# Softmax exps on VectorE as two fp16 parts from any key tile, seven P buffers, group sums turned first, new clocks in the static scheduler

## The chip, the cores and the metric

The kernel runs on one core of one Trainium2 chip. The metric is the device time of one execution in microseconds (us). Executions over 1.5% slower than the fastest of the same kernel are left out of the means. A run's ratio is the mean time of its executions over the mean time of the executions of the kernel before in the same rounds on the same chip, so it is not quite the ratio of the medians quoted beside it. One execution of the kernel before took 3638 us (its other runs 962 to 968); its cause is not known, and it is in no ratio.

## The reference, cut to what matters

```python
def _A_ref(x, wqkv, wo):                       # x: 1 x 2048 x 512, 32 heads of 16
    ...
    scores = jnp.einsum("bhqd,bhkd->bhqk", q, k) * (Dh ** -0.5)
    p = _softmax(scores, axis=-1)
    o = jnp.einsum("bhqk,bhkd->bhqd", p, v)
    ...
h = x + _A_ref(_layernorm(x), A_wqkv, A_wo)
h2 = h + _B_ref(_layernorm(h), B_w_gate, B_w_up, B_w_down)   # sigmoid-gated, width 1792
```

The work is 2048 score blocks of 128 keys x 512 queries (4 query chunks x 32 heads x 16 key tiles). Each needs an exp of 65,536 numbers and a product with V.

## The kernel before

The score matmul gives scores for 128 keys and 512 queries in PSUM. A tile is three such blocks. ScalarE takes the exp of two or three of them into a buffer `pt` ("P buffer"); VectorE may take the third. P V matmuls then add into one PSUM bank `acc`, four heads side by side in the columns. A group is 4 heads of one chunk: 64 blocks. When a group is complete, VectorE transposes `acc` and the next group may use it. Projections and the feed-forward of the previous chunk fill PE in between.

The order of all instructions is fixed when the program is built. A small scheduler in Python keeps one clock for each engine (`T["P"]`, `T["A"]`, `T["D"]` for PE, ScalarE, VectorE), adds an assumed duration for each job, and emits what its clocks say is ready. The program never changes this order afterwards, so a wrong duration can become a wait.

```python
LAT = 100.0                                   # assumed semaphore latency, ns
...
def want_dve(n):                              # shall VectorE get a block of this tile?
    ...
    if not half and len(quads) > 1: return False
    if pend > 2000 or busy > 1500: return False
    return pend + busy + 2400 + 1100 * (4 - len(half[1:])) <= rest * 1100
...
def dexp_first(src, u, n):                    # scores -> fp16 bit pattern of about 2**x
    first = nc.vector.tensor_scalar(out=J[:, k, :], in0=src, scalar1=ZOFF, scalar2=0.0,
                                    op0=ALU.add, op1=ALU.max)
    T["D"] = max(T["D"], sc_end[n] + LAT) + 610
    ...
def dexp_rest():                              # four blocks ("quad") at once, later
    X = dvx.tile([P, 3, 4, QC], I16, name="X", bufs=2)
    for s in range(1, 4):
        ... nc.vector.tensor_scalar(out=X[:, s - 1, 0:k, :], in0=J[:, 0:k, :],
                                    scalar1=float(STEP[s]), scalar2=None, op0=ALU.add)
...
# main loop, one tile n
start = max(T["A"], sc_end[n] + LAT)
dable = (len(tl) == GU and tl[-1][:2] not in ((0, 0), (0, 1)) and tl[-1][2] >= KD0   # last 5 key tiles
         and not any(un.n in hold for un in avq))
split = (dable and max(T["D"], sc_end[n] + LAT) <= start + 600 and (half or len(quads) <= 1)
         and pend <= 2000)
wa = len(tl) - split
ex = nc.scalar.activation(out=pt[:, 0:wa, :], in_=pss[:, 0:wa, :], func=ACT.Exp, scale=AS)
T["A"] = start + 98 + 427 * wa
...
if split:
    dexp_first(pss[:, GU - 1, :], tl[-1], n)
```

A VectorE block is thus a sum of four shifted fp16 patterns, each with its own weighted V (`Vw`, for the last five key tiles only, ND = 5): four P V matmuls.

## Time and profile before

| | before |
|---|---|
| median time (first three runs) | 966.4 us (962.8 to 967.7) |
| steady part (first three-block exp to last exp) | 816 us of a span of 960 us |
| ScalarE work in it at its own pace | 719 us |
| VectorE blocks / P V matmuls | 428 / 3332 |

How to read it: in the trace, exps that wait for nothing start 904 ns apart (two blocks) or 1330 ns apart (three), tanh 478 ns. "Work at its own pace" is the count of each in the steady part times these spacings; what is left of the stretch is lost to waits (97 us here). The prediction below cuts the steady part at 96 and 883 us and so gets 690 of 787 us, with the same 97 us lost.

The page of the kernel before: busy time of each engine, then tenths of busy time in 40 slices and the granted PE clock in tenths, then the chain of work that ended last.

```profile
PE 796.9 (83%) x6441; PEld 248.0 (26%) x6441; DVE 681.1 (71%) x1260; ACT 796.2 (83%) x782; POOL 2.9 (0%) x7
...
PE   4587988887878779989988888898988689799597
...
DVE  7752978777878768886767797787666697676241
ACT  5389989989989789999887898999887799898041
...
PEclk9699989989989799998997999999899799999899
...
ACT 36%; PE 35%; issue 15%; DVE 11%; DMA 1%; SPq 0%; ACTq 0%; DVEq 0%
```

ScalarE and PE are both at 83%, the chain alternates between them, and PEclk shows slices with less than the full clock.

The costliest groups of the page: line, engine, operation, out<-in, shapes and count, then busy us and mean ns, then the idle time before them and who ended it.

```profile
L1145 ACT ACTIVATE pt<-PS 128x1024 f16<-128x1024 f32 (+1 forms) x664 | 729.2, 1221 | 75.6 <-PE PS L997 55.6
L1016 DVE TENSOR_SCALAR J<-PS 128x512 int16<-128x512 f32 x428 | 289.4, 686 | 154.8 <-PE PS L905 142.8
L997 PE MATMUL PS<-pt,Vaug 128*17 128x512 f16 x1562 | 228.8, 409 | 10.3 <-DVE xs L951 10.1
L1038 DVE TENSOR_SCALAR X<-J 128x2048 int16<-128x2048 int16 (+2 forms) x351 | 211.4, 640 | 1.5
L997 PE MATMUL PS<-X,Vw 128*17 128x512 f16 x1284 | 155.9, 391 | 1.6 <-DVE X L1038 1.4
L997 PE MATMUL PS<-J,Vaug 128*17 128x512 f16 x440 | 133.3, 407 | 0.0
```

A VectorE block costs one J and three quarters of an X operation on four blocks, and the P V matmuls over J and X (1284 + 440 = 1724 recorded) outnumber those over `pt`.

Waits, total us, times, longest:

```profile
DVE J L1016 <- PE PS L905: 142.8, 159, 5.3
...
ACT pt L1145 <- PE PS L997: 55.6, 45, 3.9
...
ACT xr L1235 <- PE PS L1232: 25.3, 1, 25.3
...
ACT pt L1145 <- PE PS L905: 18.1, 36, 1.2
```

Exp waits for P V (a P buffer is not free) 55.6 us. The 25.3 us wait at L1235 is ScalarE at the very end of attention, waiting for PE.

The windows view, one row for start, steady part and tail: length, then busy us (and count) of PE, PEld, DVE, ACT, POOL, then PE clock, DMA share, GB/s.

```profile
0.00:65.40 65.40, 39.10 (x231) 16.20 (x235) 48.17 (x134) 36.58 (x47) 2.90 (x7) 0.87 0.31 97
65.40:881.60 816.20, 697.77 (x5934) 205.54 (x5927) 609.02 (x1081) 741.11 (x704) 0.00 (x0) 0.94 0.06 19
881.60:960.10 78.50, 60.01 (x281) 26.28 (x280) 23.95 (x47) 18.54 (x32) 0.00 (x0) 0.94 0.18 59
```

### The profile page before, as it was taken

Reading aid. Unit: us, or ns where it says so; the run is one execution under the profiler, and the core shown is the slowest. Engines: PE = TensorE matmul, PEld = TensorE weight load, DVE = VectorE, ACT = ScalarE, POOL = GpSimd, SP = SyncE. Lnnn points to the kernel's source line nnn. Section 1 sums busy time; section 2 is a strip of 40 time slices with the busy share of each in tenths; the row PEclk is TensorE's granted clock in tenths of the full one; section 3 lists DMA queues with packets and bytes.
Section 4 is the critical chain, followed back from the end, with each engine's and each line's share of the span. In section 5 each row is a group of like instructions: output and inputs, shape, how many; then the busy total and the mean of one; then the engine's idle time right before and its main releaser. Section 6 shows DMA issues by size and latency. Waiting matters only on the chain.

```text
span 960.1 us, 16077 instructions
## 1 busy us (share of the span) xinstructions
PE 796.9 (83%) x6441; PEld 248.0 (26%) x6441; DVE 681.1 (71%) x1260; ACT 796.2 (83%) x782; POOL 2.9 (0%) x7
## 2 busy tenths in 40 slices
PE   4587988887878779989988888898988689799597
PEld 1232222222222222222222222222222122222243
DVE  7752978777878768886767797787666697676241
ACT  5389989989989789999887898999887799898041
POOL 1000000000000000000000000000000000000000
PEclk9699989989989799998997999999899799999899
DMA  5020001000000000100000001111000000102300
GB/s 186 5 74 1 2 5 52 1 1 1 1 1 12 1 23 23 56 23 24 28 6 7 17 1 46 34 38 52 23 12 12 12 2 23 45 24 88 104 6 25
DMA packets 37169, 26.26 MB, mean 27 GB/s; under 512 B 2528, under 2 KB 37088, under 8 KB 37088
## 3 DMA queue, kind: packets, MB, share of 16 engines
q1 hardware_dynamic: 35456, 23.99, 8.3%
q10 hardware_dynamic: 1632, 1.18, 0.4%
q8 instruction: 52, 0.85, 0.4%
q14 instruction: 29, 0.24, 0.1%
HBM read 23.07 MB, written 2.10 MB: 26 GB/s over the span
## 4 chain that ended last, share of the span: by engine, by line
ACT 36%; PE 35%; issue 15%; DVE 11%; DMA 1%; SPq 0%; ACTq 0%; DVEq 0%
ACT pt L1145 34%; PE PS L997 11%; PE PS L905 10%; PE PS L695 6%; PE PS L712 4%; DVE J L1016 3%; DVE X L1038 3%; PE PS L1284 1%; ACT th L723 1%; PE PS L266 1%; DVE xs L951 1%; PE PS L261 1%; DVE st L239 1%; DMA out_dram<-ob 1%; DVE hT L707 1%
## 5 line engine op out<-in xcount | busy, mean ns | idle before, releaser
L1145 ACT ACTIVATE pt<-PS 128x1024 f16<-128x1024 f32 (+1 forms) x664 | 729.2, 1221 | 75.6 <-PE PS L997 55.6
L1016 DVE TENSOR_SCALAR J<-PS 128x512 int16<-128x512 f32 x428 | 289.4, 686 | 154.8 <-PE PS L905 142.8
L997 PE MATMUL PS<-pt,Vaug 128*17 128x512 f16 x1562 | 228.8, 409 | 10.3 <-DVE xs L951 10.1
L1038 DVE TENSOR_SCALAR X<-J 128x2048 int16<-128x2048 int16 (+2 forms) x351 | 211.4, 640 | 1.5
L997 PE MATMUL PS<-X,Vw 128*17 128x512 f16 x1284 | 155.9, 391 | 1.6 <-DVE X L1038 1.4
L997 PE MATMUL PS<-J,Vaug 128*17 128x512 f16 x440 | 133.3, 407 | 0.0
L695 PE MATMUL PS<-xnT_80,wgu 128*128 128x512 bf16 x336 | 87.9, 384 | 1.2 <-ACT th L723 0.7
L997 PEld LDWEIGHTS <-Vaug 128*17 128x17 bf16 x2048 | 56.5, 90 | 88.5 <-issue 71.3
L707 DVE SCALAR_TENSOR_TENSOR hT<-th,PS 128x512 bf16<-128x512 f32 x56 | 38.4, 686 | 29.5 <-PE PS L695 28.6
L997 PEld LDWEIGHTS <-Vw 128*17 128x17 bf16 x1284 | 39.5, 88 | 70.8 <-issue 57.1
L905 PE MATMUL PS<-QT_91,KT_85 32*128 32x512 bf16 x256 | 36.4, 408 | 18.6 <-ACT pt L1145 18.6
L723 ACT ACTIVATE th<-PS 128x512 f32<-128x512 f32 x56 | 36.0, 643 | 16.9 <-PE PS L695 16.7
L905 PE MATMUL PS<-QT_92,KT_86 32*128 32x512 bf16 x256 | 37.2, 408 | 14.9 <-ACT pt L1145 14.4
L905 PEld LDWEIGHTS <-KT_84 32*128 32x128 bf16 x512 | 21.4, 91 | 104.3 <-issue 100.2
L712 PE MATMUL PS<-wd,hT 128*128 128x512 bf16 x168 | 45.9, 404 | 2.4 <-DVE ob L717 1.6
L905 PEld LDWEIGHTS <-KT_85 32*128 32x128 bf16 x512 | 20.8, 91 | 100.8 <-issue 100.2
L905 PE MATMUL PS<-QT_90,KT_85 32*128 32x512 bf16 x256 | 36.2, 405 | 12.8 <-ACT pt L1145 12.5
L905 PEld LDWEIGHTS <-KT_86 32*128 32x128 bf16 x512 | 21.5, 91 | 93.6 <-issue 92.7
L905 PE MATMUL PS<-QT_95,KT_87 32*128 32x512 bf16 x256 | 35.9, 398 | 11.1 <-ACT pt L1145 10.7
L905 PE MATMUL PS<-QT_93,KT_86 32*128 32x512 bf16 x256 | 34.8, 389 | 11.8 <-ACT pt L1145 11.3
L905 PEld LDWEIGHTS <-KT_87 32*128 32x128 bf16 x512 | 20.1, 91 | 90.6 <-issue 90.2
L905 PE MATMUL PS<-QT_94,KT_87 32*128 32x512 bf16 x256 | 34.3, 382 | 10.8 <-ACT pt L1145 10.5
(217 smaller groups left out, 525.4 us busy)
## 6 DMA issues: line engine op xcount, KB each, us to landing
wgu<-in_B_w_gate_dram SPq DMA_DIRECT2D x21, 256.0 KB, 3.0
wgu<-in_B_w_up_dram SPq DMA_DIRECT2D x21, 256.0 KB, 3.4
out_dram<-ob SPq DMA_DIRECT2D x16, 128.0 KB, 1.7
wd<-in_B_w_down_dram SPq DMA_DIRECT2D x1, 1792.0 KB, 7.6
xr<-in_A_x_dram SPq DMA_DIRECT2D x12, 128.0 KB, 2.6
X<-in_B_w_gate_dram SPq DMA_DIRECT2D x2, 768.0 KB, 4.6
X<-in_B_w_up_dram SPq DMA_DIRECT2D x2, 768.0 KB, 6.3
wv_sb<-in_A_wqkv_dram SPq DMA_DIRECT2D x1, 512.0 KB, 6.0
```

The lines of the kernel that those rows point to most:

```text
L239: nc.vector.bn_stats(out=st[:], in_=src)
L261: nc.tensor.matmul(ps, lhsT=w_sb[:, d, p * P:(p + 1) * P], rhs=xnT[c][:, d, :], start=(d == 0), stop=(d == DC - 1))
L266: nc.tensor.matmul(ps, lhsT=xnT[t // TQ][:, d, (t % TQ) * P:(t % TQ + 1) * P], rhs=wv_sb[:, d, :], start=(d == 0), stop=(d == DC - 1))
L695: nc.tensor.matmul(ps, lhsT=w[:, d, :], rhs=hnT[:, d, :], start=(d == 0), stop=(d == DC - 1))
L707: nc.vector.scalar_tensor_tensor(out=hT[:, f, :], in0=th[:], scalar=1.0, in1=ps, op0=ALU.add, op1=ALU.mult)
L712: nc.tensor.matmul(ps, lhsT=hT[:, f, i * P:(i + 1) * P], rhs=wd[:, f, :], start=(f == 0), stop=(f == FC - 1))
L723: nc.scalar.activation(out=th[:], in_=ps, func=ACT.Tanh, scale=0.5)
L905: mm = nc.tensor.matmul(pss[:, ui, :], lhsT=KT[g // 2][32 * j:32 * j + 32, kt * P:(kt + 1) * P], rhs=q[32 * j:32 * j + 32, :], start=True, ...
L997: nc.tensor.matmul(acc[32 * j:32 * j + VW, :], lhsT=v, rhs=un.ap, start=(c == 0), stop=(todo[qc, g, j] == 0), tile_position=(0, 32 * j))
L1016: first = nc.vector.tensor_scalar(out=J[:, k, :], in0=src, scalar1=ZOFF, scalar2=0.0, op0=ALU.add, op1=ALU.max)
L1038: nc.vector.tensor_scalar(out=X[:, s - 1, 0:k, :], in0=J[:, 0:k, :], scalar1=float(STEP[s]), scalar2=None, op0=ALU.add)
L1145: ex = nc.scalar.activation(out=pt[:, 0:wa, :], in_=pss[:, 0:wa, :], func=ACT.Exp, scale=AS)
```

## The change

The intent: (1) a VectorE block becomes two parts instead of four, so it needs two P V matmuls; no weighted V is needed, so any key tile may go to VectorE; (2) the freed SBUF holds seven P buffers instead of five; (3) the transpose of the group's sums goes ahead of other VectorE jobs; (4) the scheduler's clocks get new values (an exp 904 or 1330.5 ns, a tanh 478 ns, as spaced in the trace; the latencies and tails are settings for which no measurement stands here) and now foresee the wait for a P buffer. A block is J = 2^e(1+f) as fp16; the parts are about 2^e and 0.5·2^e(1+f)², which together follow the exponential.

```diff
-    ptp = ...tile_pool(name="ptp", bufs=5)
+    ptp = ...tile_pool(name="ptp", bufs=7)
-    Vw = const.tile([P, 3, ND, H, VW], BF16)
...
-    LAT = 100.0
+    LAT = 60.0
+    TAIL = {"A": 150.0, "D": 85.0}
-            self.end = T[eng]
+            self.end = T[eng] + TAIL[eng]
-    DRAIN = 150.0
+    DRAIN = 170.0
...            (about twenty job durations, for example)
-                pm_out(dve(1150, lambda i=i, pt=pt: nc.vector.tensor_copy(
+                pm_out(dve(605, lambda i=i, pt=pt: nc.vector.tensor_copy(
-            job = pm_out(dve(700, add, st["mark"]))
+            job = pm_out(dve(603, add, st["mark"]))
...
-            out=xs..., in_=acc), Mark(T["P"]))
+            out=xs..., in_=acc), Mark(T["P"] + DRAIN), pr=-1)
...
-        X = dvx.tile([P, 3, 4, QC], I16, name="X", bufs=2)
-        for s in range(1, 4): ... op0=ALU.add
+        X = dvx.tile([P, 2, 4, QC], I16, name="X", bufs=XB)          # XB = 3
+        def power():      X[:, 0] = (J & 0x7C00) | 7                  # tensor_scalar, four blocks
+        def fraction():   X[:, 1] = (J & 0x3FF) | 0x3800              # tensor_scalar, four blocks
+        def product(a, b): X[:, 1, a:b] = J[a:b] * X[:, 1, a:b]       # tensor_tensor fp16, two blocks
...
-        if pend > 2000 or busy > 1500:
+        if pend > 2600 or busy > 1500:
-        return pend + busy + 2400 + 1100 * (4 - len(half[1:])) <= rest * 1100
+        return pend + busy + 3000 + 1100 * (4 - len(half[1:])) <= rest * 1100
...
         start = max(T["A"], sc_end[n] + LAT)
+        if n - NPT not in hold:
+            start = max(start, av_end.get(n - NPT, 0.0) + LAT)
-        dable = (len(tl) == GU and tl[-1][:2] not in ((0, 0), (0, 1)) and tl[-1][2] >= KD0
+        dable = (len(tl) == GU and tl[-1][:2] not in ((0, 0), (0, 1))
...
-        split = (... and (half or len(quads) <= 1) and pend <= 2000)
+        split = (... and (half or (len(quads) < XB and len(open_j) < JB)) and pend <= 2600)
...
-        T["A"] = start + 98 + 427 * wa
+        T["A"] = start + 51 + 426.5 * wa
```

(The bodies of `power`, `fraction` and `product` are shortened to what they compute. The loads of the last chunk's gate weights into these buffers move behind the last P V matmuls but one tile.)

More of the change, by code (lines that the diff above doesn't have):

```diff
@@ L23 @@
 LOG2E = 1.4426950408889634
-STEP = (0, 258, 512, 770)
-WEIGHT = (1.0, 0.83984375, 0.70703125, 0.59375)
-LEVEL = 2.056638710885438
+POWER, LITTLE = 0x7C00, 7
+FRACTION, HALF = 0x3FF, 0x3800
+LEVEL = 0.5910364375591628
 SUM_LOW, SUM_HIGH = 256.0, 60000.0
@@ L171 @@
     PSUM = bass.MemoryType.PSUM
-    ND = 5
-    KD0 = NT - ND
     ZS = 1024 * SC * LOG2E
@@ L187 @@
     otp = main.enter_context(tc.tile_pool(name="otp", bufs=6))
-    ptp = main.enter_context(tc.tile_pool(name="ptp", bufs=5))
+    ptp = main.enter_context(tc.tile_pool(name="ptp", bufs=7))
     dvx = main.enter_context(tc.tile_pool(name="dvx", bufs=1))
@@ L270, in v_out @@
         nc.vector.tensor_copy(out=Vaug[:, t, :, 0:DH], in_=ps.rearrange("p (h d) -> p h d", d=DH))
-    def v_weigh(t, s):
-        nc.vector.tensor_scalar(out=Vw[:, s - 1, t - KD0], in0=Vaug[:, t], scalar1=WEIGHT[s],
-                                scalar2=None, op0=ALU.mult)
     def split_q(dst, a, qd):
@@ L550, in prep_v @@
         v_mm(ps, t)
-        job = pm_out(dve(640, lambda: v_out(ps, t), st["mark"]))
-        jobs = [job] + [dve(230, lambda s=s: v_weigh(t, s), job) for s in range(1, 4) if t >= KD0]
-        done["v", t] = jobs
+        done["v", t] = [pm_out(dve(603, lambda: v_out(ps, t), st["mark"]))]
     def early_ln(c):
@@ L567, in early_ln @@
         for i in range(TQ):
-            ja.append(dve(335, lambda i=i: apply(c, i), jn, After(("x", c - 1, i // 2)), pr=pr))
+            ja.append(dve(325, lambda i=i: apply(c, i), jn, After(("x", c - 1, i // 2)), pr=pr))
         def turn():
@@ L591, in early_k @@
                              start=(d == 0), stop=(d == DC - 1))
-        done["k0", c] = [pm_out(dve(640, lambda: nc.vector.tensor_copy(
+        done["k0", c] = [pm_out(dve(603, lambda: nc.vector.tensor_copy(
             out=KT[0][:, c * QC:(c + 1) * QC], in_=ps), st["mark"]))]
@@ L599, in prep_k @@
             proj8(ps, wk_sb, p, c)
-            done["k", p] = [pm_out(dve(640, lambda ps=ps, c=c: nc.vector.tensor_copy(
+            done["k", p] = [pm_out(dve(603, lambda ps=ps, c=c: nc.vector.tensor_copy(
                 out=KT[p][:, c * QC:(c + 1) * QC], in_=ps), st["mark"]))]
@@ L608, in prep_q @@
         dst = QTb if (qc, p) == (1, 0) else QT[2 * p:2 * p + 2]
-        job = pm_out(dve(640, lambda: nc.vector.tensor_scalar(
+        job = pm_out(dve(603, lambda: nc.vector.tensor_scalar(
             out=qd[:], in0=ps, scalar1=ZS, scalar2=None, op0=ALU.mult), st["mark"]))
-        done["q", qc, p] = [dve(220, lambda a=a: split_q(dst, a, qd), job) for a in range(2)]
+        done["q", qc, p] = [dve(262, lambda a=a: split_q(dst, a, qd), job) for a in range(2)]
     OT, otj = {}, {}
@@ L671, in add @@
                     XR.append(load_xr(qc, i + 2))
-            job = pm_out(dve(700, add, st["mark"]))
+            job = pm_out(dve(603, add, st["mark"]))
             bs = new_st()
-            j = dve(660, lambda i=i, bs=bs: stats1(h[:, i, :], bs), job)
-            j = dve(180, lambda i=i, bs=bs: stats2(bs, mv[:, i, :]), j)
+            j = dve(605, lambda i=i, bs=bs: stats1(h[:, i, :], bs), job)
+            j = dve(100, lambda i=i, bs=bs: stats2(bs, mv[:, i, :]), j)
         jn = newton_jobs(rstd[:], mv[:, :, 1], j)
@@ L683, in wo_ln @@
         for i in range(2):
-            jh[i] = dve(420, lambda i=i: apply(i), jn)
+            jh[i] = dve(455, lambda i=i: apply(i), jn)
         for i in range(TQ):
@@ L687, in wo_ln @@
             pt = transpose4(pm_tile(), hns[i])
-            pm_out(dve(440, lambda pt=pt, i=i: nc.vector.tensor_copy(
+            pm_out(dve(335, lambda pt=pt, i=i: nc.vector.tensor_copy(
                 out=hnT[:, :, i * P:(i + 1) * P], in_=pt), st["mark"]))
             if i + 2 < TQ:
-                jh[i + 2] = dve(420, lambda i=i: apply(i + 2), jn, st["mark"])
+                jh[i + 2] = dve(455, lambda i=i: apply(i + 2), jn, st["mark"])
     def gate_mm(ps, w):
@@ L738, in ffn_up @@
         gate_mm(ps, wgu[:, 0])
-        ja = pm_out(act(530, lambda: th.update({f: tanh_out(ps)}), st["mark"]))
+        ja = pm_out(act(478, lambda: th.update({f: tanh_out(ps)}), st["mark"]))
         yield pe(4, pm_new)
@@ L748, in ffn_up @@
                 GW.append(load_gate(f + 3 - FC))
-        pm_out(dve(700, lambda: glu_out(hT, f, th[f], ps2), st["mark"], ja))
+        pm_out(dve(603, lambda: glu_out(hT, f, th[f], ps2), st["mark"], ja))
     def ffn_down(qc, i):
@@ L760, in ffn_down @@
             down_mm(ps, hT, i, f, f + n)
-        pm_out(dve(700, lambda: down_out(ps, qc, i), st["mark"]))
+        pm_out(dve(603, lambda: down_out(ps, qc, i), st["mark"]))
     HOLD = Mark(None)
@@ L829, with __init__ @@
     class Block:
-        def __init__(self, qc, g, kts, kds):
+        def __init__(self, qc, g, kts):
             self.qc, self.g = qc, g
             self.a = {j: deque(kts) for j in range(4)}
-            self.d = {j: deque(kds) for j in range(4)}
         def left(self):
-            return sum(len(q) for q in (*self.a.values(), *self.d.values()))
-    blocks = deque(Block(0, g, range(c * TQ, (c + 1) * TQ), ()) for g, c in early)
-    blocks.extend(Block(qc, g, range(KD0), range(KD0, NT)) for qc, g in gseq[2:])
+            return sum(len(q) for q in self.a.values())
+    blocks = deque(Block(0, g, range(c * TQ, (c + 1) * TQ)) for g, c in early)
+    blocks.extend(Block(qc, g, range(NT)) for qc, g in gseq[2:])
     tiles = []
@@ L851, in pick @@
         if want:
-            js = [j for j in range(4) if b.d[j]]
-            if js:
-                j = max(js, key=lambda j: (len(b.d[j]), -((j - st["dj"]) % 4)))
-                last = (b.qc, b.g, b.d[j].popleft(), j)
+            j = st["dj"] % 4
+            if b.a[j]:
+                last = (b.qc, b.g, b.a[j].popleft(), j)
                 st["dj"] = j + 1
@@ L859, in pick @@
             b = blocks[0]
-            for pool in (b.a, b.d):
-                js = [j for j in range(4) if pool[j]]
-                if js:
-                    break
-            else:
+            js = [j for j in range(4) if b.a[j]]
+            if not js:
                 blocks.popleft()
@@ L869, in pick @@
                 continue
-            j = max(js, key=lambda j: (j not in used, len(pool[j]), -((j - st["aj"]) % 4)))
-            out.append((b.qc, b.g, pool[j].popleft(), j))
+            j = max(js, key=lambda j: (j not in used, len(b.a[j]), -((j - st["aj"]) % 4)))
+            out.append((b.qc, b.g, b.a[j].popleft(), j))
             st["aj"] = j + 1
@@ L914, with __init__ @@
     class Unit:
-        def __init__(self, u, ap, n, end, s=0):
-            self.u, self.ap, self.n, self.end, self.s, self.d = u, ap, n, end, s, -1
+        def __init__(self, u, ap, n, end):
+            self.u, self.ap, self.n, self.end, self.d = u, ap, n, end, -1
     avq = []
+    av_end = {}
     count, todo = {}, {}
@@ L922 @@
             count[qc, g, j], todo[qc, g, j] = 0, NT
-    NPT = 5
+    NPT = 7
     def finish_group(qc, g):
@@ L950, in turn @@
                     queue(ffn_down(qc, i), ("d", qc, i), 14 * ((qc, i) != (NQC - 2, TQ - 1)))
-        j = st["acc"] = dve(730, lambda: nc.vector.transpose(
-            out=xs[:].rearrange("p b r -> p (b r)"), in_=acc), Mark(T["P"]))
-        j = dve(680, norm, j)
+        j = st["acc"] = dve(650, lambda: nc.vector.transpose(
+            out=xs[:].rearrange("p b r -> p (b r)"), in_=acc), Mark(T["P"] + DRAIN), pr=-1)
+        j = dve(620, norm, j)
         if a:
-            otj[qc, p] = dve(720, turn, j)
+            otj[qc, p] = dve(630, turn, j)
     def av_last():
@@ L995, in av @@
             h = 8 * (g // 2) + 2 * j + g % 2
-            v = Vaug[:, kt, h, :] if un.s == 0 else Vw[:, un.s - 1, kt - KD0, h, :]
-            nc.tensor.matmul(acc[32 * j:32 * j + VW, :], lhsT=v, rhs=un.ap, start=(c == 0),
+            nc.tensor.matmul(acc[32 * j:32 * j + VW, :], lhsT=Vaug[:, kt, h, :], rhs=un.ap, start=(c == 0),
                              stop=(todo[qc, g, j] == 0), tile_position=(0, 32 * j))
         pe_time("av", MM * rows + 4 * len(uns))
+        for un in uns:
+            if un.d < 0:
+                av_end[un.n] = T["P"] + DRAIN
         qc, g = uns[0].u[:2]
@@ L1004, in av @@
         return len(uns)
-    JB = 3
-    quads = []
+    JB, XB = 2, 3
+    quads, open_j = [], []
     half = []
@@ L1015, in dexp_first @@
         k = len(half) - 1
-        first = nc.vector.tensor_scalar(out=J[:, k, :], in0=src, scalar1=ZOFF, scalar2=0.0,
-                                        op0=ALU.add, op1=ALU.max)
-        T["D"] = max(T["D"], sc_end[n] + LAT) + 610
-        todo[u[0], u[1], u[3]] += 3
-        uns = [Unit(u, J[:, k, :].bitcast(FP16), n, T["D"])]
-        uns += [Unit(u, None, n, None, s) for s in range(1, 4)]
+        nc.vector.tensor_scalar(out=J[:, k, :], in0=src, scalar1=ZOFF, scalar2=0.0,
+                                op0=ALU.add, op1=ALU.max)
+        T["D"] = max(T["D"], sc_end[n] + LAT) + 601
+        todo[u[0], u[1], u[3]] += 1
+        uns = [Unit(u, None, n, None) for s in range(2)]
         for un in uns:
@@ L1028, in dexp_first @@
             dexp_rest()
-        return first
     def dexp_rest():
@@ L1034, in dexp_rest, with ready, power, fraction @@
         k = len(quad)
-        X = dvx.tile([P, 3, 4, QC], I16, name="X", bufs=2)
-        for s in range(1, 4):
-            def step(s=s):
-                nc.vector.tensor_scalar(out=X[:, s - 1, 0:k, :], in0=J[:, 0:k, :],
-                                        scalar1=float(STEP[s]), scalar2=None, op0=ALU.add)
-                for i, uns in enumerate(quad):
-                    uns[s].ap, uns[s].end = X[:, s - 1, i, :].bitcast(FP16), T["D"]
-            chain.append((70 + 133 * k, step))
+        X = dvx.tile([P, 2, 4, QC], I16, name="X", bufs=XB)
+        V = nc.vector
+        open_j.append(J)
+        def ready(s, a, b):
+            for i in range(a, b):
+                quad[i][s].ap, quad[i][s].end = X[:, s, i, :].bitcast(FP16), T["D"] + TAIL["D"]
+        def power():
+            V.tensor_scalar(out=X[:, 0, 0:k, :], in0=J[:, 0:k, :], scalar1=POWER, scalar2=LITTLE,
+                            op0=ALU.bitwise_and, op1=ALU.bitwise_or)
+            ready(0, 0, k)
+        def fraction():
+            V.tensor_scalar(out=X[:, 1, 0:k, :], in0=J[:, 0:k, :], scalar1=FRACTION, scalar2=HALF,
+                            op0=ALU.bitwise_and, op1=ALU.bitwise_or)
+        def product(a, b):
+            x = X[:, 1, a:b, :].bitcast(FP16)
+            V.tensor_tensor(out=x, in0=J[:, a:b, :].bitcast(FP16), in1=x, op=ALU.mult)
+            ready(1, a, b)
+            if b == k:
+                open_j.pop(0)
+        chain.append((70 + 133 * k, fraction))
+        chain.append((70 + 133 * k, power))
+        for a in range(0, k, 2):
+            b = min(a + 2, k)
+            chain.append((70 + 267 * (b - a), lambda a=a, b=b: product(a, b)))
     def pop_chain():
@@ L1056, in want_dve @@
         rest = group_left() / 2.8
-        if not half and len(quads) > 1:
+        if not half and (len(quads) >= XB or len(open_j) >= JB):
             return False
-        if pend > 2000 or busy > 1500:
+        if pend > 2600 or busy > 1500:
             return False
-        return pend + busy + 2400 + 1100 * (4 - len(half[1:])) <= rest * 1100
+        return pend + busy + 3000 + 1100 * (4 - len(half[1:])) <= rest * 1100
     slots, hold = [], {}
     def early_slots():
-        for i in range(2):
-            x = dvx.tile([P, 3, 4, QC], I16, name="X", bufs=2)
-            slots.extend(x[:, s, 2 * k:2 * k + 2, :] for s in range(3) for k in range(2))
-        for i in range(JB):
-            x = dvx.tile([P, 4, QC], I16, name="J", bufs=JB)
-            slots.extend(x[:, 2 * k:2 * k + 2, :] for k in range(2))
-        slots.extend(prep.tile([P, 2, QC], I16, name=f"hold{i}")[:] for i in range(5))
+        for name, b in (("X", XB), ("J", JB)):
+            for i in range(b):
+                x = dvx.tile([P, 2, 4, QC] if name == "X" else [P, 4, QC], I16, name=name, bufs=b)
+                for s in range(2):
+                    slots.extend(([x[:, s, 0:2, :], x[:, s, 2:4, :]]) if name == "X" else [x[:, 2 * s:2 * s + 2, :]])
+        slots.extend(prep.tile([P, 2, QC], I16, name=f"hold{i}")[:] for i in range(7))
     def pt_tile(n):
@@ L1132 @@
         start = max(T["A"], sc_end[n] + LAT)
+        if n - NPT not in hold:
+            start = max(start, av_end.get(n - NPT, 0.0) + LAT)
         busy = sum(j.ns for j in dq if j.ready() is not None)
         pend = sum(c[0] for c in chain)
-        dable = (len(tl) == GU and tl[-1][:2] not in ((0, 0), (0, 1)) and tl[-1][2] >= KD0
+        dable = (len(tl) == GU and tl[-1][:2] not in ((0, 0), (0, 1))
                  and not any(un.n in hold for un in avq))
-        split = (dable and max(T["D"], sc_end[n] + LAT) <= start + 600 and (half or len(quads) <= 1)
-                 and pend <= 2000)
+        split = (dable and max(T["D"], sc_end[n] + LAT) <= start + 600 and (half or (len(quads) < XB and len(open_j) < JB))
+                 and pend <= 2600)
         if half and half[1][0].u[:2] != tl[-1][:2]:
@@ L1141 @@
             quads[:] = [q for q in quads if any(un in avq for un in q)]
-            split = split and len(quads) <= 1
+            split = split and len(quads) < XB and len(open_j) < JB
         wa = len(tl) - split
@@ L1145 @@
         ex = nc.scalar.activation(out=pt[:, 0:wa, :], in_=pss[:, 0:wa, :], func=ACT.Exp, scale=AS)
-        T["A"] = start + 98 + 427 * wa
-        ex_end[n] = T["A"]
-        avq.extend(Unit(u, pt[:, ui, :], n, T["A"]) for ui, u in enumerate(tl[:wa]))
+        T["A"] = start + 51 + 426.5 * wa
+        ex_end[n] = T["A"] + TAIL["A"]
+        avq.extend(Unit(u, pt[:, ui, :], n, ex_end[n]) for ui, u in enumerate(tl[:wa]))
         if split:
             dexp_first(pss[:, GU - 1, :], tl[-1], n)
-            ex_end[n] = max(ex_end[n], T["D"])
+            ex_end[n] = max(ex_end[n], T["D"] + TAIL["D"])
         run_act()
@@ L1191 @@
     flush()
-    tw = {}
-    Xs = [dvx.tile([P, 3, 4, QC], I16, name="X", bufs=2) for i in range(2)]
-    Js = dvx.tile([P, 4, QC], I16, name="J", bufs=JB)
-    for i, (t, f, n) in enumerate(((Xs[0], 0, 6), (Xs[1], 6, 6), (Js, 12, 2))):
-        w = t[:].rearrange("p a b n -> p (a b n)") if n == 6 else t[:].rearrange("p b n -> p (b n)")
-        w = w.bitcast(BF16).rearrange("p (k c n) -> p k c n", k=2, c=DC)
-        for k in range(2):
-            nc.sync.dma_start(out=w[:, k], in_=gate_v[k][:, :, f * P:(f + n) * P])
-        for m in range(n):
-            tw[f + m] = w[:, :, :, m * P:(m + 1) * P]
     while bg and HOLD not in (bg[0][2] or pe(0))[2]:
@@ L1207 @@
         av(8, 1e12)
+    tw = {}
+    for i in range(XB + JB):
+        t = (dvx.tile([P, 2, 4, QC], I16, name="X", bufs=XB)[:].rearrange("p a b n -> p (a b n)") if i < XB
+             else dvx.tile([P, 4, QC], I16, name="J", bufs=JB)[:].rearrange("p b n -> p (b n)"))
+        n = min(4 if i < XB else 2, FC - len(tw))
+        f = len(tw)
+        w = t[:, 0:n * 2 * DC * P].bitcast(BF16).rearrange("p (k c n) -> p k c n", k=2, c=DC)
+        for k in range(2):
+            nc.sync.dma_start(out=w[:, k], in_=gate_v[k][:, :, f * P:(f + n) * P])
+        for m in range(n):
+            tw[f + m] = w[:, :, :, m * P:(m + 1) * P]
+        if len(tw) == FC:
+            break
     qc = NQC - 1
```

## The prediction

> **What bounds it now.** From the windows view, three parts: start to 96 us (tiles two blocks wide), a steady part 96–883 us (tiles of three 128x512 score blocks), and a tail 883–960 us. The steady part decides. In the trace, back-to-back exps on ScalarE start 904 ns (two blocks) or 1330 ns (three blocks) apart, tanh 478 ns. All ScalarE work of the steady part at these spacings adds to 690 of 787 us: ScalarE is the bound at 88%, and 97 us are lost to waits. The waits view names them: exp waiting for the P V matmuls (a P buffer not yet free) 55.6 us in 45 waits, up to 3.9 us each; waiting for scores 18 us. Counted per group (between two transposes of the P V accumulator), the loss is 4 to 8 us in groups that change over badly or carry much feed-forward work. VectorE is 71% busy; PE is 83% busy but its matmul times overlap, so that is no peak.
>
> **What the change does.**
> - P V: a VectorE block needs two matmuls instead of four. The before has 428 such blocks (count of J), 3332 P V matmuls. Four run side by side, and a row of four takes about 0.216 us, so 856 fewer matmuls free about 46 us of PE, 50 us with the mean granted clock. This shortens its catching up at group changes and in the feed-forward groups.
> - Seven P buffers: two more tiles (about 2 us) of slack against the 55.6 us wait. I expect this to pay directly. Turning the accumulator first helps the same place.
> - VectorE per block: before, J 601 ns (start to start) + 3 x 600/4 = 1.05 us. After, J 601 + two bit operations on four blocks, 2 x 600/4, + two products on two blocks each. [...]
> - So the number of VectorE blocks hardly grows. Any key tile may go there, [...] and the start rule near a group's end is stricter. I expect 400 to 460 blocks (14 a group, as before); each block more or less moves 0.43 us of ScalarE.
>
> **Sum.** Steady ScalarE work stays 690 us (±12). Loss falls from 97 to about 45 us. Start 96 us and tail 77 us change little (−2). 96 + 735 + 77 − 2 ≈ 906; with a reserve for a later VectorE (it holds the score bank), 912 us.
>
> Range 885 to 943 us. Faster by over 2%: 0.85; within 2%: 0.12; slower: 0.03.
>
> **What would show it.** Waits of exp for P V matmuls under 20 us in all; P V matmuls about 2048 + J count; 128x2048 bit operations with a duration near 690 ns[...]; J count 400–460; steady ScalarE spacing unchanged at 904/1330[...].
>
> **What would make it wrong.** [...] VectorE saturating so that J comes late and score banks stall PE and ScalarE; J count well under 400 (ScalarE floor up) or well over 470 (a bigger gain); lower granted clock; new clocks in the scheduler that are too eager, so in-order PE stalls on not-yet-ready parts.

Cut from it, where marked, is the author's reckoning of what a VectorE block costs after the change, with what hung on it (a product, the VectorE work in all, its busy share, a quad): it was not worked out from the traces of this case. What it says of P V matmuls is in the trace of before: those of a row start about 4 ns apart and rows 216 to 221 ns apart (5th percentile and median), and the 1562 over `pt`, 409 ns each or 639 us in all, keep PE busy for only 228.8 us.

## The result, and the profile after

The kernel after takes 902.5 us (901.75 to 907.41, four runs) against 966.8 us, ratio 0.9353 with a 95% interval of 0.9311 to 0.9396: 6.5% faster, and within the predicted range. The parts of the sum are another matter:

| profiled run, us | before | after | predicted |
|---|---|---|---|
| start, to the first three-block exp | 65.3 | 66.6 | start and tail together −2 |
| steady: ScalarE work at its own pace | 718.7 | 692.3 | unchanged, ±12 |
| steady: lost to waits | 97.4 | 85.2 | −52 |
| tail, after the last exp | 78.6 | 55.8 | start and tail together −2 |
| VectorE blocks | 428 | 487 | 400 to 460 |

```profile
PE 765.6 (85%) x5644; PEld 232.0 (26%) x5644; DVE 795.4 (88%) x1470; ACT 770.8 (86%) x783; POOL 2.9 (0%) x7
...
PE   4498888877787899999998989989978898989897
...
DVE  7742899999999899999998999999999999899832
ACT  5399998989989999999898999988898998899741
...
PEclk9699998899988999999997899999998999899999
...
DVE 37%; ACT 26%; PE 23%; issue 12%; DMA 0%; ACTq 0%; DVEq 0%
```

VectorE went from 71% to 88% busy and now leads the chain that ended last (37%); before it had 11%.

```profile
L1155 ACT ACTIVATE pt<-PS 128x1024 f16<-128x1024 f32 (+1 forms) x663 | 700.8, 1169 | 60.3 <-PE PS L985 38.6
L1007 DVE TENSOR_SCALAR J<-PS 128x512 int16<-128x512 f32 x487 | 324.6, 685 | 16.2 <-PE PS L893 9.1
L985 PE MATMUL PS<-pt,Vaug 128*17 128x512 f16 x1499 | 218.4, 406 | 7.0 <-DVE xs L940 6.8
L1043 DVE TENSOR_TENSOR X<-J,X 128x1024 f16<-128x1024 f16 (+1 forms) x251 | 161.7, 669 | 0.0
L985 PE MATMUL PS<-X,Vaug 128*17 128x512 f16 x1014 | 150.9, 396 | 6.5 <-DVE X L1033 4.7
...
L1038 DVE TENSOR_SCALAR X<-J 128x2048 int16<-128x2048 int16 (+3 forms) x133 | 85.3, 642 | 0.2
L1033 DVE TENSOR_SCALAR X<-J 128x2048 int16<-128x2048 int16 (+3 forms) x133 | 85.2, 640 | 0.0
```

Back to back, the new operations start about 600 ns apart, as J does: the two bit operations on four blocks (2048 elements) 599 and 601 ns, products on two blocks (1024 elements) 601 ns, J 601 ns; the add on 2048 elements in before had 601.5 ns. Durations are 685 to 687 ns (the means above mix in smaller shapes). So a block in a full quad costs 601 + 2 x 600/4 + 601/2, about 1.2 us (an estimate from these spacings), against 1.05 us before. But there are 487 J.

```profile
ACT pt L1155 <- PE PS L985: 38.6, 26, 5.2
...
ACT pt L1155 <- PE PS L893: 19.2, 33, 1.8
...
DVE J L1007 <- PE PS L893: 9.1, 18, 1.3
...
ACT xr L1249 <- PE PS L1246: 4.0, 1, 4.0
```

VectorE no longer waits for scores (142.8 us before, 9.1 now): it is late itself. Exp still waits 38.6 us for P V; the prediction wanted under 20. The wait at the end of attention (xr) is gone.

```profile
0.00:66.50 66.50, 40.83 (x239) 15.90 (x239) 43.67 (x116) 38.20 (x48) 2.90 (x7) 0.87 0.29 95
66.50:844.10 777.60, 676.33 (x5182) 194.79 (x5185) 730.98 (x1315) 714.72 (x705) 0.00 (x0) 0.95 0.07 21
844.10:900.00 55.90, 48.41 (x231) 21.35 (x230) 20.72 (x41) 17.92 (x32) 0.00 (x0) 0.94 0.19 61
```

The tail has 231 matmuls where it had 281: the rest of the third chunk's feed-forward (12 gate or up and 56 down matmuls in the order of instructions of before, 14 down now) is done before attention ends.

**A late VectorE, seen in one place.** For each tile whose third block goes to VectorE, J and the exp of the other two blocks read the same score tile, whose banks the program gives to new scores only after both (in after the score matmuls waited 82.3 us in 195 waits for an exp of `pt`, and 0.2 us in one wait for J). In before, J ended after that exp in 22 of 428 tiles, 2.5 us in all; in after, in 179 of 487, 40.3 us in all. The timeline of after around one group change (start, us, engine, line, operation):

```profile
643.61 0.71 PE L985 MATMUL PS<-X,Vaug 128*17 128x512 f16 x2 [0.21 <-DVE X L1033]
...
643.81 0.69 DVE L1007 TENSOR_SCALAR J<-PS 128x512 int16<-128x512 f32 x1
...
644.25 0.67 PE L893 MATMUL PS<-QT_88,KT_84 32*128 32x512 bf16 x6
644.53 0.69 DVE L1038 TENSOR_SCALAR X<-J 128x2048 int16<-128x2048 int16 x1
...
645.14 0.68 DVE L1007 TENSOR_SCALAR J<-PS 128x512 int16<-128x512 f32 x1
645.74 0.68 DVE L1033 TENSOR_SCALAR X<-J 128x2048 int16<-128x2048 int16 x1
...
646.34 0.69 DVE L1007 TENSOR_SCALAR J<-PS 128x512 int16<-128x512 f32 x1
...
646.94 0.71 DVE L940 STREAM_TRANSPOSE xs<-PS 128x512 f32<-128x512 f32 x1
...
647.70 0.39 PE L985 MATMUL PS<-pt,Vaug 128*17 128x512 f16 x3 [0.25 <-DVE xs L940]
647.70 0.11 PEld L985 LDWEIGHTS <-Vaug 128*17 128x17 bf16 x7 [0.24 <-issue]
...
648.17 2.37 ACT L1155 ACTIVATE pt<-PS 128x1536 f16<-128x1536 f32 x2 [1.49 <-PE PS L985]
...
648.37 1.89 PE L259 MATMUL PS<-xnT_83,wq_sb 128*128 128x512 bf16 x4
```

The last two P V matmuls of the group (643.61) end at 644.32. The transpose of the sums could follow, but VectorE still has J, a bit operation, J, a bit operation and J in its fixed order, and starts the transpose at 646.94. The next group's P V matmuls begin only at 647.70, P buffers run out, and the exp at 648.17 has waited 1.49 us. Then four projection matmuls (648.37) take 1.89 us where four of the same line took 1.04 us at 351.53 us: the clock record has 0.5 from 648.1 us on. In after, gaps of ScalarE over 0.3 us from 3 us before to 4 us after such a transpose add to about 45.6 us (some us more or less, by how gaps at the edge are counted).

### The profile page after: what moved, and what is told of

Read it like the earlier page. It is cut to its first block, busy times and chain, and to the rows that moved or that the text cites. A ratio compares the mean times of both kernels' runs of the same rounds, so it can differ in the third digit from the quotient of the medians.

```text
span 900.0 us, 14693 instructions
## 1 busy us (share of the span) xinstructions
PE 765.6 (85%) x5644; PEld 232.0 (26%) x5644; DVE 795.4 (88%) x1470; ACT 770.8 (86%) x783; POOL 2.9 (0%) x7
## 4 chain that ended last, share of the span: by engine, by line
DVE 37%; ACT 26%; PE 23%; issue 12%; DMA 0%; ACTq 0%; DVEq 0%
ACT pt L1155 23%; DVE J L1007 15%; DVE X L1043 7%; PE PS L688 6%; PE PS L985 5%; PE PS L893 5%; DVE X L1033 4%; DVE X L1038 3%; DVE xs L940 2%; PE PS L264 1%; DVE hT L700 1%; PE PS L1298 1%; PE PS L259 1%; PE PS L705 1%; ACT th L716 1%
## 5 line engine op out<-in xcount | busy, mean ns | idle before, releaser
L1155 ACT ACTIVATE pt<-PS 128x1024 f16<-128x1024 f32 (+1 forms) x663 | 700.8, 1169 | 60.3 <-PE PS L985 38.6
L1007 DVE TENSOR_SCALAR J<-PS 128x512 int16<-128x512 f32 x487 | 324.6, 685 | 16.2 <-PE PS L893 9.1
L985 PE MATMUL PS<-pt,Vaug 128*17 128x512 f16 x1499 | 218.4, 406 | 7.0 <-DVE xs L940 6.8
L1043 DVE TENSOR_TENSOR X<-J,X 128x1024 f16<-128x1024 f16 (+1 forms) x251 | 161.7, 669 | 0.0
L985 PE MATMUL PS<-X,Vaug 128*17 128x512 f16 x1014 | 150.9, 396 | 6.5 <-DVE X L1033 4.7
L985 PEld LDWEIGHTS <-Vaug 128*17 128x17 bf16 x2535 | 63.6, 89 | 151.5 <-issue 130.3
L1038 DVE TENSOR_SCALAR X<-J 128x2048 int16<-128x2048 int16 (+3 forms) x133 | 85.3, 642 | 0.2
L1033 DVE TENSOR_SCALAR X<-J 128x2048 int16<-128x2048 int16 (+3 forms) x133 | 85.2, 640 | 0.0
L893 PE MATMUL PS<-QT_90,KT_85 32*128 32x512 bf16 x256 | 39.5, 428 | 12.5 <-ACT pt L1155 12.0
L893 PE MATMUL PS<-QT_93,KT_86 32*128 32x512 bf16 x256 | 37.8, 397 | 10.1 <-ACT pt L1155 9.5
L893 PE MATMUL PS<-QT_92,KT_86 32*128 32x512 bf16 x256 | 37.2, 381 | 10.4 <-ACT pt L1155 9.9
L893 PE MATMUL PS<-QT_91,KT_85 32*128 32x512 bf16 x256 | 36.4, 395 | 11.1 <-ACT pt L1155 10.5
L893 PE MATMUL PS<-QT_94,KT_87 32*128 32x512 bf16 x256 | 35.4, 384 | 11.3 <-ACT pt L1155 11.0
L893 PEld LDWEIGHTS <-KT_84 32*128 32x128 bf16 x512 | 20.5, 91 | 92.0 <-issue 87.3
L705 PE MATMUL PS<-wd,hT 128*128 128x512 bf16 x168 | 43.9, 382 | 0.4 <-DVE ob L710 0.4
L893 PE MATMUL PS<-QT_95,KT_87 32*128 32x512 bf16 x256 | 37.0, 392 | 8.0 <-ACT pt L1155 7.6
L893 PEld LDWEIGHTS <-KT_85 32*128 32x128 bf16 x512 | 20.4, 92 | 89.4 <-issue 88.1
L893 PEld LDWEIGHTS <-KT_86 32*128 32x128 bf16 x512 | 20.2, 91 | 84.7 <-issue 84.4
L893 PEld LDWEIGHTS <-KT_87 32*128 32x128 bf16 x512 | 19.4, 91 | 84.2 <-issue 83.2
```

The lines of the kernel that those rows point to most:

```text
L705: nc.tensor.matmul(ps, lhsT=hT[:, f, i * P:(i + 1) * P], rhs=wd[:, f, :], start=(f == 0), stop=(f == FC - 1))
L893: mm = nc.tensor.matmul(pss[:, ui, :], lhsT=KT[g // 2][32 * j:32 * j + 32, kt * P:(kt + 1) * P], rhs=q[32 * j:32 * j + 32, :], start=True, ...
L985: nc.tensor.matmul(acc[32 * j:32 * j + VW, :], lhsT=Vaug[:, kt, h, :], rhs=un.ap, start=(c == 0), stop=(todo[qc, g, j] == 0), tile_positio ...
L1033: V.tensor_scalar(out=X[:, 0, 0:k, :], in0=J[:, 0:k, :], scalar1=POWER, scalar2=LITTLE, op0=ALU.bitwise_and, op1=ALU.bitwise_or)
L1038: V.tensor_scalar(out=X[:, 1, 0:k, :], in0=J[:, 0:k, :], scalar1=FRACTION, scalar2=HALF, op0=ALU.bitwise_and, op1=ALU.bitwise_or)
L1043: V.tensor_tensor(out=x, in0=J[:, a:b, :].bitcast(FP16), in1=x, op=ALU.mult)
```

## The experiments

The theories. **A** (the prediction): fewer waits for P buffers, from buffers and PE relief, are the gain. **B**: the gain is ScalarE work moved to VectorE, and a shorter tail from the new clocks. C to I came up on the way. All runs gave correct results. "Blocks" is the number of VectorE blocks; half-clock is the time for which the trace's clock record, which holds only 1.0 and 0.5, has 0.5 in the profiled run.

| run | median us | ratio | blocks | P V matmuls | steady work + lost, us | tail us | half-clock us |
|---|---|---|---|---|---|---|---|
| before | 966.8 | 1 | 428 | 3332 | 718.7 + 97.4 | 78.6 | 120.6 |
| after | 902.5 | 0.9353 | 487 | 2535 | 692.3 + 85.2 | 55.8 | 110.6 |
| u1 five buffers | 919.8 | 0.9552 | 500 | 2548 | 686.7 + 108.2 | 55.1 | 100.2 |
| u2 old clocks | 965.0 | 1.0021 | 468 | 2516 | 699.8 + 103.8 | 96.1 | 195.7 |
| u3 sums not first | 901.6 | 0.9348 | 490 | 2538 | 691.0 + 86.0 | 56.5 | 100.8 |
| u4 old key tiles | 890.9 | 0.9246 | 426 | 2474 | 718.3 + 53.1 | 54.2 | 144.2 |
| u5 none at a group's end | 895.1 | 0.9274 | 419 | 2467 | 721.3 + 49.4 | 56.2 | 121.3 |
| u6 every third given back | 874.3 | 0.9040 | 415 | 2463 | 723.0 + 27.6 | 56.1 | 73.8 |
| u7 before + new clocks | 895.4 | 0.9279 | 447 | 3389 | 709.3 + 62.6 | 54.2 | 58.8 |
| u8 leftover put back | 916.5 | 0.9505 | 488 | 2536 | 691.9 + 85.1 | 64.7 | 119.4 |
| v1 u7, every sixth given back | 904.6 | 0.9396 | 418 | 3302 | 721.7 + 56.8 | 55.1 | 52.7 |
| v2 before + new latencies | 913.0 | 0.9472 | 440 | 3368 | 712.3 + 70.0 | 61.5 | 73.2 |
| v3 before + new durations | 925.0 | 0.9599 | 441 | 3371 | 711.4 + 67.2 | 78.2 | 92.8 |
| v4 every fourth given back | 880.4 | 0.9145 | 454 | 2502 | 706.4 + 48.7 | 54.3 | 74.3 |

### u1: five buffers

```diff
-    ptp = ...tile_pool(name="ptp", bufs=7)
+    ptp = ...tile_pool(name="ptp", bufs=5)
-    NPT = 7
+    NPT = 5
```

> The kernel after with five P buffers instead of seven, nothing else. The order of instructions holds 500 VectorE blocks (487 in after) and no more leftover feed-forward work. Theory A (the prediction: the buffers pay directly, because ScalarE waits for a free P buffer): exp waits for P V matmuls rise from 38.6 us to 60 us or more, time 915 to 930 us. Theory B (the gain is ScalarE work moved to VectorE and a shorter tail; the wait for P V comes from late group ends, which buffers only delay): time 900 to 910 us.

919.8 us, ratio 0.9552 (0.9517 to 0.9586). Exp waited 68.7 us for P V (38.6 in after). Theory A holds for this part: two buffers are worth 17 us in this kernel. The scheduler also answered with 13 more VectorE blocks, so it is not the buffers with all else fixed. The same step on the kernel before could not be built: without the change's smaller tables the build with seven buffers stops at the pool `fwork`, which needs 8 kb a partition where 5.78 kb are left (with six it builds; that was not run).

### u2: the old clocks

```diff
-    LAT = 60.0; TAIL = {"A": 150.0, "D": 85.0}; DRAIN = 170.0
+    LAT = 100.0; DRAIN = 150.0                  # and no tails
-        if n - NPT not in hold:
-            start = max(start, av_end.get(n - NPT, 0.0) + LAT)
-        T["A"] = start + 51 + 426.5 * wa
+        T["A"] = start + 98 + 427 * wa
...                                              # and all job durations as in before
```

> The kernel after with all scheduler times of before (latencies, tails, durations, no predicted P-buffer wait), nothing else. The order of instructions holds 468 VectorE blocks (19 fewer, 8 us more ScalarE), and after the last scores 40 more gate or up matmuls and 42 more down matmuls of the third chunk, as in before. If the clocks matter through the tail (theory B): the time from the last exp to the end grows from 56 us to 72 to 80 us and the whole is 920 to 935 us. If the clocks are only cosmetics (theory A): within 5 us of after.

965.0 us, ratio 1.0021: the whole gain is gone, more than theory B expected. The tail grew to 96 us, the steady part to 804 us, and PE spent 196 us at half clock. So of the 62 us, 40 are in the tail and 26 in the steady part (start is 3 us shorter). The tail is worse than that of before (79 us): after the last exp the trace has 39 gate or up and 55 down matmuls of the third chunk, against 8 and 56 in before and 14 down in after.

### u3: group sums not turned first

```diff
-..., in_=acc), Mark(T["P"] + DRAIN), pr=-1)
+..., in_=acc), Mark(T["P"] + DRAIN))
```

> The kernel after with the transposes of the group sums queued behind other VectorE jobs, as in before, nothing else. 490 VectorE blocks. Both theories: 0 to +6 us; PE waits for the accumulator (6.8 us in after) rise to about 10 us as in before.

901.6 us, ratio 0.9348: no difference. PE's wait for the transpose rose from 6.8 to 9.4 us, but it cost nothing. The timeline above suggests why the step does little: it puts the transpose ahead of other queued jobs, not ahead of J and the quad's operations that are already emitted. The run shows one thing more: here J ended after its exp in only 120 of 490 tiles, 22.4 us in all (179 and 40.3 us in after), and the steady part lost the same 86 us. So a late J is a sign of the overload, not a measure of what it costs.

### u4: VectorE blocks from the last five key tiles only

```diff
+    ND = 5; KD0 = NT - ND                       # key tiles of a group in two pools, as in before
...                                              # and the pools in Block and pick
-        dable = (len(tl) == GU and tl[-1][:2] not in ((0, 0), (0, 1))
+        dable = (len(tl) == GU and tl[-1][:2] not in ((0, 0), (0, 1)) and tl[-1][2] >= KD0
```

> The kernel after with VectorE blocks only from the last five key tiles, as in before, nothing else. The order of instructions holds 426 VectorE blocks instead of 487: 61 more on ScalarE, 26 us more ScalarE work at 0.4265 us each. Theory B: 915 to 930 us, and VectorE busy falls to about 80%. Theory A (count of blocks does not matter, waits do): within 8 us of after.

890.9 us, ratio 0.9246 (0.9224 to 0.9268): *faster* than after. Both theories fall here. ScalarE had 26 us more work, exactly as counted, but lost 32 us less, and exp waited 12.9 us for P V. The freedom of the key tile, the headline of the change, costs about 12 us as this scheduler uses it. The code says how the count rises: the limit to five key tiles also kept VectorE from taking blocks that `want_dve` had not asked for; without it, `split` takes any tile for which the clocks leave room. Building the orders again and counting bears this out: 59 of 428 blocks had not been asked for in before, 189 of 487 in after, 64 of 426 in u4. (An order built with `split` bound to `want_dve` has 374 blocks; it was not run.)

### u5 and u6: is it the place of the blocks, or their number?

u5, no block for VectorE when fewer than 12 of the group are left:

```diff
+        left_after.append(sum(b.left() for b in blocks if (b.qc, b.g) == tiles[n][-1][:2]))
-        dable = (len(tl) == GU and
+        dable = (len(tl) == GU and left_after[n] >= 12 and
```

> The kernel after, any key tile, but no VectorE block once fewer than 12 score blocks of the group are left. The order of instructions holds 419 VectorE blocks (487 in after; 426 in the run with the old key tiles, which was 12 us faster than after). Theory C (VectorE blocks late in a group make the group's sums late, so ScalarE runs out of P buffers at each group change): 885 to 895 us, gaps near a group change about half of the 45.6 us of after. Theory D (the freedom of the key tile itself costs, place and count do not): within 4 us of after.

u6, every third block given back, wherever it falls:

```diff
+        st["even"] = st.get("even", 0) + split
+        split = split and st["even"] * 1 % 3 >= 1
```

> The kernel after, any key tile, with every third VectorE block given back to ScalarE wherever it falls. The order holds 415 VectorE blocks, as many as the run that keeps them off the last 12 blocks of a group, but also at the group's end. Theory C (place): slower than that run by 6 us or more, gaps near a group change stay above 35 us. Theory E (count alone: VectorE is overloaded with 487): within 3 us of that run.

u5 took 895.1 us, ratio 0.9274, and u6 874.3 us, ratio 0.9040 (0.8990 to 0.9090). With 419 and 415 blocks they differ by 21 us, and against theory C the one that still takes blocks at a group's end wins. Theory E (number alone) falls as well, since the numbers are nearly equal. (u5 by itself had looked like C, at the edge of its 885 to 895 us, and not like theory D, that the freedom of the key tile itself costs. Against D speaks also that u6, with any key tile, is 17 us faster than u4 with five.) What differs is how the load is spread. The count of tiles whose J ends after their exp is 179 of 487 in after, 57 of 419 in u5 (11.6 us) and 26 of 415 in u6 (2.9 us); gaps near a group change add to about 45.6, 19.3 and 2.5 us. Busy time and chain of u6, from its page, then its waits:

```profile
PE 744.7 (85%) x5572; PEld 228.6 (26%) x5572; DVE 718.7 (82%) x1325; ACT 795.9 (91%) x783; POOL 2.9 (0%) x7
...
ACT 51%; PE 23%; issue 18%; DVE 6%; DMA 1%; SPq 0%; ACTq 0%; DVEq 0%
```

```profile
DVE J L1007 <- PE PS L893: 51.1, 83, 2.2
...
ACT pt L1157 <- PE PS L893: 8.2, 24, 0.9
...
PE PS L985 <- DVE xs L940: 0.9, 2, 0.5
```

From the view of the tile `pt` on ScalarE in u6, what the exps waited for (us, times):

```profile
its engine sat idle before it (us, times) until:
  PE PS L893: 8.2, 24
...
  PE PS L985: 0.3, 1
```

The wait of exp for P V, 38.6 us in after, is 0.3 us in u6, once. ScalarE leads the chain with 51%, VectorE has 6%. That a regular three-block exp gives VectorE and PE time to catch up is the explanation I argue for, and no run shows it by itself; shown is that VectorE is on time, that the loss near group changes is gone, and that PE is at half clock for 74 us instead of 121 us in u5. The clock is a rival that was not separated: 47 us less at half clock are worth up to 23 us of full-speed PE (an estimate, half of 47), as much as the whole difference, and no run tells whether the even load or the clock came first.

### v4: every fourth block given back

```diff
+        st["even"] = st.get("even", 0) + split
+        split = split and st["even"] * 1 % 4 >= 1
```

> The kernel after, any key tile, every fourth VectorE block given back: 454 blocks, between the 487 of after (902 us) and the 415 with every third left out (874 us). Theory E (load of VectorE is what counts, with a threshold near its free time): 876 to 890 us. If 415 was already below the best count: 870 us or less, the best of all.

880.4 us, ratio 0.9145 (0.9116 to 0.9174), within the range that theory E gave (a threshold itself was not measured). It has 17 us less ScalarE work than u6 and loses 21 us more. So of these two counts 415 is the better, and u6 stays the best kernel. It also limits the explanation by regular pauses: from 100 us after the start to 70 us before the end, VectorE worked for over 10 us without a pause of 0.1 us in 30% of the time in u6, 43% in u5 and 58% in after, but in 67% in v4, which is faster than u5.

### u7, v2, v3: the new clocks on the kernel before

u7 takes the kernel before and changes only the scheduler's numbers (and the predicted P-buffer wait); v2 only latencies, tails, exp times and that wait; v3 only the job durations.

> The kernel before with the new scheduler times alone (latencies, tails, durations, the predicted P-buffer wait), four-part exps, five P buffers, old key tiles. The order holds 447 VectorE blocks (428 in before) and no leftover of the third chunk's feed-forward after the last scores beyond 14 down matmuls. If the clocks carry most of the gain by themselves: 915 to 935 us, tail 56 us. If they pay only together with the two-part exps (PE or VectorE too full without them): 945 us or more.

> The kernel before with only the latencies, tails, exp times and the predicted P-buffer wait of the new clocks, job durations as before. 440 VectorE blocks, 38 down matmuls left over after the last scores. All new clocks together gave 895 us. Theory H (latencies and the P-buffer wait are the effective part): 900 to 918 us. Theory I (job durations are): 945 us or more.

> The kernel before with only the new job durations on VectorE and ScalarE (640 to 603 ns for an eviction, 1150 to 605 for the early transposed copy and so on), latencies as before. 441 VectorE blocks, 8 gate or up and 56 down matmuls left over, as in before. Theory H: 950 us or more. Theory I: 900 to 925 us.

u7 took 895.4 us, ratio 0.9279 (0.9237 to 0.9320): better than expected, and at least as fast as the kernel after (0.9311 to 0.9396). The clocks alone are worth 7.2%, the whole change 6.5%. v2 gave 913.0 us (0.9472), v3 925.0 us (0.9599). Neither theory H nor I is right: each half gains by itself, 5.3% and 4.0%, and together less than their sum. v2 shortened the tail by 17 us, v3 left it as it was (78.2 us); both cut the loss in the steady part from 97 to about 70 us.

### u8: the leftover put back into the tail

```diff
-                yield pe(n, pm_new, HOLD if (qc, i) == (NQC - 2, TQ - 1) else None)
+                yield pe(n, pm_new, HOLD if (qc, i) == (NQC - 2, TQ - 1) else HOLD2 if qc == NQC - 2 else None)
...
     N = len(tiles)
+    HOLD2.end = 0.0
```

> The kernel after with 42 down matmuls of the third chunk held back until attention has ended, which makes the tail do what it did in before. 488 VectorE blocks. If the tail explains its 23 us by this work: the stretch after the last exp grows by 10 to 16 us (before needed about 15 us for 12 gate or up and 56 down matmuls there), the steady part shortens by 0 to 5 us, the whole is 908 to 918 us. If the work only moves: within 3 us of after.

916.5 us, ratio 0.9505 (0.9475 to 0.9535), 14 us more than after. Its profiled run was its fastest (909.3 us; the others 914.9 to 917.1 us); in it the tail grew by 8.9 us to 64.7 us while the steady part stayed at 777 us. So leftover feed-forward at the end is paid in full (42 matmuls of about 0.216 us are 9.1 us, an estimate). The rest of the 14 us is not in the profiled run and stays open. The leftover makes up for 9 us of the 23 us directly; the other changes of the tail were not tried one by one.

### v1: what the two parts themselves are worth

u7 with every sixth block given back has as many VectorE blocks as u6, but four parts each.

```diff
             split = split and len(quads) <= 1
+        st["even"] = st.get("even", 0) + split
+        split = split and st["even"] * 1 % 6 >= 1
```

> The kernel before with the new scheduler times (895 us in its run) and every sixth VectorE block given back: 418 blocks, as many as the 415 of the two-part kernel with every third left out (874 us), but four P V matmuls a block (3302 in all, 2463 there) and five P buffers. Theory F (the two-part exps pay once VectorE is not overfilled: 839 fewer P V matmuls, about 45 us of PE): 885 us or more, and more half-clock or P V waits than the 874 us kernel. Theory G (the parts are worth nothing here, only the clocks and an even load are): 870 to 880 us.

904.6 us, ratio 0.9396, against 0.9040 of u6: theory F holds. Exp waited 26.7 us for P V; half clock was not more than in u6 (53 and 74 us), which theory F had left open. With four parts, giving blocks back makes the kernel slower than u7; its chain has PE at 40%, ScalarE at 37% and VectorE at 8%, and VectorE waited 96.0 us for scores (51.1 us in u6). So two parts with what they bring (839 fewer P V matmuls and room for two more buffers) are worth about 30 us at this count of blocks, and 21 us between the fastest kernel of each kind (u6 and u7); in after, with VectorE at 88% busy, nothing is left of it. u1 puts some 17 us of it to the buffers in another setting; the two were not separated here, and the way the blocks are thinned (one in six, one in three) differs too.

## Why the prediction was right or wrong

The total, 912 us in a range of 885 to 943, was right (902.5), but by luck: the sum behind it came out because its errors cancelled. ScalarE work was 26 us under the forecast, the loss 40 us over it, start and tail 20 us under it.

- **Right:** ScalarE's own work fills most of the steady part (692.3 of 777.5 us); its spacings stayed at 904 and 1330 ns. The bit operations on 2048 elements have the duration foreseen, near 690 ns (685 and 687 measured); a product of 1024 elements takes as long (685 ns, starts 601 ns apart). P V matmuls are 2048 plus the J count. Two buffers pay, 17 us.
- **Mis-sized, the VectorE blocks:** "the number of VectorE blocks hardly grows ... 400 to 460". It grew to 487. I took `want_dve` for the rule that limits them, but what held the number down in before was the key-tile condition in `dable`: `want_dve` did ask for fewer (298 blocks in the built order, 369 before), and 189 came in unasked (59 before). This took 26.4 us off ScalarE instead of 0 ± 12 and put VectorE at 88% busy (71% before).
- **Failed, the loss:** "Loss falls from 97 to about 45 us". It fell to 85, and exp waited 38.6 us for P V, not under 20. The prediction named the risk, "VectorE saturating so that J comes late and score banks stall PE and ScalarE", and its first part came: J ended after its exp in 179 tiles, and group sums were turned late. A stall of PE on J's score banks is not in the trace beyond the 0.2 us above. With an even load (u6) the loss is 27.6 us, less than was predicted.
- **Failed, the tail:** "tail 77 us change little". It fell by 23 us. u7 shows that the clocks alone do this (54.2 us); u8 that work put back into it is paid.
- **Failed by omission, the clocks:** the sum has no term for them; they appear only as a risk ("too eager"). They are worth 62 us inside this kernel (u2) and 69 us on the kernel before (u7).
- **Failed, small:** "Turning the accumulator first helps": nothing was seen (u3).

Step by step, the change is a 7% gain from the clocks, a gain from two parts and buffers (21 to 30 us where VectorE has room) that the overfilled VectorE uses up, and nothing from the order of the sums. The best version found is u6, 9.6% under before and 3.3% under after by the ratios (0.9040 to 0.9353).

**Why the new clocks matter so much** is shown in part. The trace's clock record changes in steps of 3.41 us. I cut the record into windows of that length and took all full-clock ones, from 100 us after the start to 70 us before the end of all 14 profiled runs, and the share of each in which matmuls were busy. After a window under 0.6, the next one was at half clock in 91 of 104 cases; after one of 0.6 to 0.65, in 28 of 66; after one over 0.75, in 6 of 2261. Of 152 ends of half clock, 147 came after a window that was over 0.9 busy. The median window is about 0.9 busy. So in these traces a window in which PE was idle for more than about 1.4 us of 3.41 us (a share under 0.6) was mostly followed by 3.4 us or more at half clock. In after no long single gap came before it: in the steady part the longest gap of PE in the 6.8 us before a half-clock stretch was 0.2 to 1.0 us. Whether half clock in turn brings further waits was not measured. The totals fit: 196 us at half clock with the old clocks (u2), 59 us with the new (u7). It is not the whole story: u4 had 144 us of half clock and was faster than after with 111 us.

## What to carry to other kernels

Where a kernel's order comes from a model of the engines, measure the model's durations first; here that was worth more than the new arithmetic, and it must be tried alone before a larger change gets the credit. Work moved to another engine can become too much for it: here 415 VectorE blocks gave 874.3 us, 454 gave 880.4 us and 487 gave 902.5 us. Watch when the engine finishes against the one that it relieves, not its busy share alone, and leave it slack (here every third block given back did best). A condition that looks like a data restriction (here the key tile) can be the load limiter; count the work after removing it.
